# Score masks before the last two multiplications of a group, and GpSimd's two scalings of a unit's q before two different steps

## The chip, the cores and the metric

The kernel runs on one core of a Trainium2 chip. The metric is device time in microseconds. One core has TensorE (matrix multiplications, called PE in the profile), VectorE (DVE), ScalarE (ACT), GpSimd (POOL) and the queue of SyncE (SP), which here only issues DMAs. Each engine works through its own instructions in the order in which the program lists them, and waits for other engines where the program says so.

## The reference

Everything is float32 at the end; the weights come in as float64.

```python
def _attn_ref(q, k, v):                      # (8, 8, 576, 64)
    B, H, S, D_ = q.shape
    scores = np.matmul(q, k.transpose(0, 1, 3, 2)) / np.sqrt(D_)
    gamma = 1.0 - 2.0 ** (-5.0 - np.arange(H, dtype=np.float32))
    rel = np.arange(S)[:, None] - np.arange(S)[None, :]
    Dmat = np.where(rel >= 0, gamma[:, None, None] ** rel[None], 0.0)
    return np.matmul(scores * Dmat[None], v)

def _moe_ref(x, w1, w2, w3, w_out):          # x: (4608, 512)
    h = (x @ w1) * (x @ w2) @ w3             # 512 -> 1024 -> 1024
    return h @ w_out                         # 1024 -> 512
```

The attention is causal with a decay by head and no softmax. Its output, heads side by side, is the x of the second block.

## The kernel before

**Attention.** The work is cut into 20 units: four pairs of batches (`NB2`) by five chunks of the sequence (`NC`; the first has 64 rows, the others 128). The decay is split into a factor on q and a factor on v, so a unit needs a scaled q and a scaled v. For a unit, `score` (L224) multiplies q and k on TensorE into four PSUM tiles `sc`, and VectorE multiplies each by the causal mask into `pm` (L236). `state` (L240) adds k^T v to a running state, and `pv` (L278) multiplies the state and the masked scores into the attention's output, which ScalarE copies out to `xT`. Units 5 to 9 and 12 to 19 bring q in as 32 x 32 blocks: `load_blocks` (L160) issues 16 small DMAs on SP, `scale_blocks` (L175) scales the tile `bl_q` on GpSimd, one instruction (L181) for each of the pair's two batches, and `front_blocks` (L185) transposes it on VectorE (L190).

**Feed-forward.** The tokens of two batches make three tiles of 384. The two first products are made with Strassen's scheme, for the later half of the tokens twice nested: `up2` (L1037) is one of 14 steps (2 halves of the width by 7 outer products) for a pair of token tiles. A step issues eight matmul groups into three PSUM tiles (`up` twice, `seed` once); ScalarE copies and VectorE adds (L1072, L1070) take them out into `cc`, and GpSimd adds parts of `cc` to others (L1065). `next_forms` (L957) issues the DMA of a later step's weights, `ra<-kept` (L961), on GpSimd's queue, into a ring of three slots. The end of a step, its last matmul group, is held in `behind` and put into the next step by `finish`. When both factors of a part are ready, `multiply` (L1024) multiplies them on VectorE into `ab` (L1032), so many as its argument allows; `results` keeps what is left. `down` (L632) takes `ab` and makes the last product, Strassen's seven products of 128 tokens by 256 columns (`po`, L651, w3 and w_out having been multiplied together before), with sums on VectorE (L614 to L620, L655, L699, L701).

**Order.** The order is written by hand; `nc`'s instructions stand on each engine as the Python emits them. The last loop runs over g from 10 to 19. In each round `work(n)` takes n entries of `todo`: 14 `up2` and then three `down` for each pair of token tiles. `dealt = [3, 4, 4, 3, 3, 7, 7, 3, 7, 7]` says how many in each round, so groups 13, 16 and 19 end with the last `up2` of a pair and groups 14 and 17 consist of the three `down`. `aside`, `beside` and `loads` are lists from which steps take one entry each: transposes, v's scalings on ScalarE, k's loads. A round ends with `pv(g)`, at groups 13, 16 and 19 (`ready`) with `finish()` and `multiply()`, then the load of v and `state(g + 1)`, `score(g + 1)`; at the ready groups `token_forms` then prepares the next pair's sums.

**PSUM.** In this part `acc` has five tiles for `up`, `sc`, `xps` and `po`, and `seed` has two. A tile is taken again once its last reader is done: the second product of the `down` that follows a score takes the tile of the first `sc`, and so waits for the first mask.

Of the kernel before, what the change touches and what calls it, by code (L numbers as in the profile page):

```python
# [19 lines left out]
def kernel(  # L20
# [66 lines left out]
    def load(g, names, engine=nc.sync):  # L87
        i, c = divmod(g, NC)
        sz = sizes[c]
        src = {"k": k, "q": q, "v": v}  # L90
        for nm in names:
            t = pools["ld"].tile([P, 2 * H, D], F32, tag="ld_" + nm, name="ld_" + nm)
            engine.dma_start(
                t[:sz], src[nm][2 * i:2 * i + 2, :, starts[c]:starts[c] + sz, :].rearrange("b h p d -> p (b h) d"))
            live[nm, g] = t
# [27 lines left out]
    for c in (0, slice(1, NC)):  # L123
        n = short if c == 0 else P
# [35 lines left out]
    def load_blocks(g, nm):  # L160

        i, c = divmod(g, NC)
        n = sizes[c] // BL
        t = pools["ld"].tile([P, 2 * NP, P // BL, BL], F32, tag="ld_q", name="bl_" + nm)
        src = {"k": k, "q": q}[nm][2 * i:2 * i + 2].rearrange("b (p a) s d -> a (b p) s d", a=2)
        for a in range(2):
            for f in range(D // BL):
                part = (a * (D // BL) + f) * BL
                for m in range(n):
                    s0 = starts[c] + m * BL  # L170
                    nc.sync.dma_start(t[part:part + BL, :, m, :],  # L171
                                      src[a, :, s0:s0 + BL, f * BL:(f + 1) * BL].rearrange("m r x -> r m x"))
        live["bl_" + nm, g] = t

    def scale_blocks(g):  # L175
        c = g % NC
        n, n0 = sizes[c] // BL, starts[c] // BL
        t = live["bl_q", g]
        for b in range(2):
            part = t[:, b * NP:(b + 1) * NP, :n, :]  # L180
            nc.gpsimd.tensor_tensor(  # L181
                out=part, in0=part, in1=gqs[:, :, n0:n0 + n].unsqueeze(3).to_broadcast([P, NP, n, BL]),
                op=ALU.mult)

    def front_blocks(g, names="kq"):  # L185
        c = g % NC
        n = sizes[c] // BL
        for nm in names:
            dst = pools["fr"].tile([P, 2, NP, P], F32, tag=nm + "T", name=nm + "T", bufs=1 if nm == "k" else 2)
            nc.vector.transpose(  # L190
                dst[:, :, :, :sizes[c]].rearrange("p b m (n x) -> p (b m) n x", x=BL),
                live["bl_" + nm, g][:, :, :n, :])
            live[nm + "T", g] = dst

    def scale(g, nm, scalar=False, engine=nc.gpsimd):
        c = g % NC
        sz = sizes[c]
        t, gam = live[nm, g], {"q": gq, "v": gk}[nm]
        t = t[:sz].rearrange("p (b h) d -> p b h d", b=2)
        if scalar:  # L200
            for h in range(H) if scalar is True else scalar:
                nc.scalar.mul(t[:, :, h, :], t[:, :, h, :], gam[:sz, c, h:h + 1])
            return
        engine.tensor_tensor(
            out=t, in0=t, in1=gam[:sz, c].unsqueeze(1).unsqueeze(3).to_broadcast([sz, 2, H, D]), op=ALU.mult)

    def front(g, names="kq"):
        c = g % NC
        sz = sizes[c]
        for nm in names:  # L210
            src = live[nm, g]
            dst = pools["fr"].tile([P, 2, NP, P], F32, tag=nm + "T", name=nm + "T",
                                   bufs=1 if nm == "k" and g >= NC else 2)
            for b in range(2):
                tp = acc.tile([P, NP, P], F32, tag="acc", name="tp")
                for p in range(NP):
                    h = b * H + 2 * p
                    nc.tensor.transpose(tp[:, p, :sz],  # L218
                                        src[:sz, h:h + 2, :].rearrange("p a d -> p (a d)"),
                                        ident[:sz, :sz])  # L220
                nc.scalar.copy(dst[:, b, :, :sz], tp[:, :, :sz])
            live[nm + "T", g] = dst
# [350 lines left out]
    g = 0  # L573
# [53 lines left out]
    def ahead(x, y, n=3):  # L627
        todo_sums = pair_of(x, y)[2]
        for _ in range(min(n, len(todo_sums))):
            aside.append(todo_sums.pop(0))  # L630
# [389 lines left out]
    def finish():  # L1020
        while behind:
            behind.pop(0)()

    def multiply(most=2 * len(order)):  # L1024
        while results and most:
            gr, h, f, b, z, s = results.pop(0)
            m = groups[gr][s]
            if ("ab", *every[m]) not in live:
                live["ab", *every[m]] = ffn.tile([P, 2 * KF, TB], F32, tag="ab", name="ab")
            ab = live["ab", *every[m]].rearrange("p (q i) t -> p q i t", i=4)[:, 2 * h:2 * h + 2, 2 * f + b, :]  # L1030
            v = z.rearrange("p (m s) w t -> p m s w t", s=2)[:, :, s]
            nc.vector.tensor_mul(ab, v[:, :, 0, :], v[:, :, 1, :])  # L1032
            if s == 0:
                free.append(z)
            most -= 1
# [94 lines left out]
    def add_group(gr):  # L1130
        X, Y = groups[gr]
        todo.extend((up2, gr, n) for n in range(14))
        todo.extend([(down, (X, 0), (X, 1)), (down, (X, 2), (Y, 2)), (down, (Y, 0), (Y, 1))])

    def work(n):
        while n > 0 and todo:
            fn, *args = todo.pop(0)

            nxt = next((x for x in todo if x[0] in real), None)
            if nxt and nxt[0] is down:  # L1140
                if fn is down:
                    args.append(nxt[1:])
                else:
                    ahead(*nxt[1:], 1 if fn is up2 else 3)
            if g == G and not todo:
                fn(*args, last=True)
            else:
                fn(*args)
            n -= 1
            while todo and todo[0][0] not in real:  # L1150
                todo.pop(0)[0]()

    g = NC
    scale_blocks(NC)
    scale(NC, "v")
    front(NC, "k")
    front_blocks(NC, "q")
    state(NC)
    score(NC)
    scale_blocks(NC + 1)  # L1160
    in_blocks = [u >= 2 * NC - 3 for u in range(G)] + [False] * 2
    first_pair = range(NC, 2 * NC - 1)
    for g in first_pair:
        n = (1, 1, 2, 2)[g - NC]
# [43 lines left out]
    g = 2 * NC - 1  # L1208
# [9 lines left out]
    g = 2 * NC  # L1218
# [15 lines left out]
    for g in range(2 * NC, G):  # L1234
        n = dealt[g - 2 * NC]
        if g + 1 < G:
            q_blocks = g > 2 * NC
            if not q_blocks:
                beside.extend(lambda j=j: scale(g + 1, "q", range(j, j + H // 2)) for j in (0, H // 2))
            tail = {3: 0, 4: 1, 7: 3}[n]  # L1240
            work(n - 2 - tail)
            beside.extend(lambda j=j: scale(g + 1, "v", range(j, j + H // 2)) for j in (0, H // 2))
            if q_blocks:
                scale_blocks(g + 1)
            for nm in "qk":
                blocks_in = q_blocks if nm == "q" else g + 1 not in whole
                if blocks_in:
                    aside.append(lambda nm=nm: front_blocks(g + 1, nm))
                work(1)
                while aside:  # L1250
                    aside.pop(0)()
                if not blocks_in and nm == "k":
                    while loads:
                        loads.pop(0)()
                    front(g + 1, "k" if q_blocks else "kq")
                if g + 2 < G and not (nm == "k" and g + 2 in whole):
                    load_blocks(g + 2, nm)
            work(tail)
            for left in (loads, beside):
                while left:  # L1260
                    left.pop(0)()
        else:
            work(n)
        pv(g)()
        if g in ready:
            finish()
            multiply()
        if g + 2 < G:
            load(g + 2, "v", nc.gpsimd)
            if (g + 2) % NC != NC - 1:  # L1270
                loads.append(lambda g=g: load(g + 2, "k", nc.gpsimd))
        if g + 1 < G:
            state(g + 1)
            score(g + 1)
        if g in ready:
            add_group(ready[g])
            token_forms(ready[g])
    g = G
# [44 lines left out]
```

## Time and profile before

| | |
|---|---|
| median of three runs | 831.94 us (831.66 to 832.31) |
| the profiled execution | 832.77 us |
| its span, first to last instruction | 831.0 us |
| instructions | 15815 |
| granted TensorE clock | 0.999 |
| VectorE, ScalarE, GpSimd busy | 547.6, 291.8, 222.3 us |
| L1032, multiplications on VectorE in the last loop | 64, median 0.55 us |
| L236, masks of 128x512 there | 32, mean 0.68 us |
| L181, scalings of q on GpSimd there | 16, mean 1.03 us |
| L1065, additions on GpSimd there | 108, mean 1.00 us |
| L961, `ra` issued on GpSimd there | 51, mean 0.57 us |

The rows from L1032 on are from the groups of the stretch from 380 to 800 us, which holds groups 11 to 19; group 10 begins at about 366 us. A row of the profile names line, engine and operation, then the tiles written and read; "idle before" is the time that the engine stood still ahead of the instruction, with who ended it. GpSimd's DMA issues take GpSimd's time[...]; SP's issues, about 0.45 us each, take only SP's.

### The profile page before, as it was taken

The page shows a single profiled execution, that of the slowest core. Times are in us where ns is not written, and L with a number is a line of the kernel's source. Part 1 is how long each engine was busy: PE and PEld are TensorE (multiplying, and loading weights), DVE is VectorE, ACT ScalarE, POOL GpSimd, SP SyncE. Part 2 cuts the span into 40 slices and gives each one's busy share as a digit, 9 for nine tenths or more (in the row PEclk, how much of TensorE's full clock was granted, in tenths as well). Part 3 has the DMA queues.
Part 4 walks back from the last instruction along what each step waited for, and adds up shares of the span by engine and source line. Part 5 has one row for each costly group of instructions (what it writes and reads, how often), then busy time and mean ns, then how long its engine had stood idle before and what let it go on. Part 6 is the DMA issues. An engine that isn't in the chain of part 4 may idle for free.

```text
span 831.0 us, 15815 instructions
## 1 busy us (share of the span) xinstructions
PE 817.5 (98%) x6117; PEld 737.0 (89%) x6117; DVE 547.6 (66%) x962; ACT 291.8 (35%) x609; POOL 222.3 (27%) x258
## 2 busy tenths in 40 slices
PE   8999999999999999999999999999999999999998
PEld 8889999744888998889999889998889998899987
DVE  4899999993544568754657755677745667646653
ACT  4787556572021111255443024341034331033300
POOL 1000000001303332125547015565006460045600
PEclk9999999999999999999999999999999999999999
DMA  9995454446237665988786347978245453146401
GB/s 191 226 224 137 79 131 134 117 126 104 99 66 195 113 151 186 266 264 206 200 228 184 92 88 209 240 224 217 56 92 180 163 191 114 36 149 214 141 26 51
DMA packets 196812, 126.96 MB, mean 153 GB/s; under 512 B 157848, under 2 KB 178456, under 8 KB 196736
## 3 DMA queue, kind: packets, MB, share of 16 engines
q1 hardware_dynamic: 168560, 50.40, 29.6%
q0 software_dynamic: 12480, 65.67, 24.3%
q10 hardware_dynamic: 15696, 9.87, 4.5%
q8 instruction: 48, 0.79, 0.4%
q14 instruction: 28, 0.23, 0.1%
HBM read 103.62 MB, written 22.28 MB: 152 GB/s over the span
## 4 chain that ended last, share of the span: by engine, by line
PE 89%; DVE 6%; DMA 2%; issue 1%; SPq 1%; ACT 1%; ACTq 0%; POOL 0%; DVEq 0%; POOLq 0%
PE po L651 24%; PE up L1060 17%; PE up L528 14%; PE seed L1060 13%; PE ps L477 7%; PE xps L299 3%; PE sc L233 3%; PE xps L274 2%; PE tp L218 2%; PE st L255 1%; SPq L171 1%; DVE pm L236 1%; DVE ab L1032 1%; PE idle L131 1%; DMA ld_v<-in_v_dram 1%
## 5 line engine op out<-in xcount | busy, mean ns | idle before, releaser
L651 PE MATMUL po<-w3o,ab 128*128 128x256 f32 x552 | 125.0, 381 | 2.3 <-DVE ot L655 1.0
L651 PEld LDWEIGHTS po<-w3o,ab 128*128 128x128 f32 x552 | 103.7, 190 | 18.9 <-DVE ot L655 2.5
L1065 POOL TENSOR_TENSOR cc<-cc 128x384 f32<-128x384 f32 x112 | 109.3, 1002 | 3.8 <-ACT cc L1083 2.4
L1072 DVE TENSOR_TENSOR cc<-seed,cc 128x384 f32<-128x384 f32 x88 | 48.7, 553 | 69.0 <-PE seed L1060 59.3
L181 POOL TENSOR_TENSOR bl_q<-bl_q,gqs 128x512 f32<-128x512 f32 (+1 forms) x26 | 26.0, 1020 | 185.8 <-DMA bl_q<-in_q_dram 182.3
L1060 PE MATMUL up<-xT,ra 128*128 128x192 f32 x384 | 73.7, 328 | 0.1
L528 PE MATMUL up<-xT,wA 128*128 128x192 f32 x384 | 70.7, 328 | 1.0 <-DVE xT L496 1.0
L236 DVE TENSOR_TENSOR pm<-sc,mask 128x512 f32<-128x512 f32 (+1 forms) x80 | 45.4, 627 | 35.1 <-PE sc L233 35.1
L1072 DVE TENSOR_TENSOR cc<-up,cc 128x384 f32<-128x384 f32 x88 | 48.5, 551 | 30.2 <-PE up L1060 21.8
L533 DVE TENSOR_TENSOR c<-up,c 128x384 f32<-128x384 f32 x80 | 44.1, 552 | 36.7 <-PE up L528 35.7
L651 PE MATMUL po<-wB,forms 128*128 128x256 f32 x288 | 65.4, 379 | 0.7 <-DVE pm L236 0.7
L528 PEld LDWEIGHTS up<-xT,wA 128*128 128x128 f32 x384 | 63.3, 190 | 2.4 <-PE up L528 1.2
L1060 PEld LDWEIGHTS up<-xT,ra 128*128 128x128 f32 x384 | 63.7, 190 | 1.4 <-DMA ra<-kept 0.4
L961 POOL DMA_DIRECT2D ra<-kept x54 | 30.5, 565 | 118.7 <-PE seed L1060 93.8
L651 PEld LDWEIGHTS po<-wB,forms 128*128 128x128 f32 x288 | 54.6, 190 | 8.4 <-DVE pm L236 1.1
L1079 ACT COPY seed<-up 128x384 f32<-128x384 f32 x56 | 25.9, 463 | 100.2 <-PE up L1060 56.6
L477 PE MATMUL ps<-wo,w3T 128*128 128x512 f32 x128 | 55.1, 592 | 0.0
L1060 PE MATMUL up<-ra 128*128 128x192 f32 x288 | 54.7, 326 | 0.0
L477 PEld LDWEIGHTS ps<-wo,w3T 128*128 128x128 f32 x128 | 24.3, 190 | 30.1 <-issue 29.7
L1060 PE MATMUL seed<-e,ra 128*128 128x192 f32 x256 | 50.9, 329 | 0.0
L1060 PEld LDWEIGHTS up<-ra 128*128 128x128 f32 x288 | 48.1, 190 | 0.1
L528 PE MATMUL up<-T,wS 128*128 128x192 f32 x256 | 46.7, 326 | 1.4 <-DVE wS L149 1.4
(134 smaller groups left out, 1479.1 us busy)
## 6 DMA issues: line engine op xcount, KB each, us to landing
ra<-kept POOLq DMA_DIRECT2D x54, 896.0 KB, 4.9
raw<-in_moe_w_dram SPq DMA_DIRECT2D x72, 128.0 KB, 3.0
bl_q<-in_q_dram SPq DMA_DIRECT2D x192, 32.0 KB, 3.3
out_dram<-ot ACTq DMA_DIRECT2D x41, 128.0 KB, 2.3
bl_k<-in_k_dram SPq DMA_DIRECT2D x136, 32.0 KB, 3.5
raw<-in_moe_w_dram SPq DMA_DIRECT2D x16, 256.0 KB, 5.4
ld_k<-in_k_dram SPq DMA_DIRECT2D x8, 512.0 KB, 6.1
raw<-in_moe_w_out_dram SPq DMA_DIRECT2D x32, 128.0 KB, 2.8
```

Of the source, the lines that this page charges most:

```text
L181: nc.gpsimd.tensor_tensor(out=part, in0=part, in1=gqs[:, :, n0:n0 + n].unsqueeze(3).to_broadcast([P, NP, n, BL]), op=ALU.mult)
L233: nc.tensor.matmul(sc[j][:sz, p, :sz], kT[hs, b, p, :sz], qT[hs, b, p, :sz], start=True, stop=True)
L236: nc.vector.tensor_mul(pm[:sz, b, j, :, :sz], sc[j][:sz, :, :sz], mask[:sz, :sz].unsqueeze(1).to_broadcast([sz, NP, sz]))
L477: nc.tensor.matmul(ps, live["w3T", ft][:, g, :], live["wo"][:, g, :], start=(g == 0), stop=(g == KF - 1))
L528: nc.tensor.matmul(ps[:, w, :], a[:, w, r, :], b[:, r, :], start=(new and w == r == 0), stop=(w == r == 1), skip_group_check=True)
L533: nc.vector.tensor_add(c[:, to], ps, c[:, sb])
L651: nc.tensor.matmul(ps[nm], a[A][:, f, :], live["W"][B][:, f, :], start=(f == 0 and not on), stop=(f == NP - 1), skip_group_check=True)
L961: engine.dma_start(ring[n % 3], kept[n % 14 // 7][nm])
L1060: nc.tensor.matmul(ps[:, w, :], weight_of(slot, a, w), B[b], start=(new and w == 0), stop=True, skip_group_check=True)
L1065: nc.gpsimd.tensor_tensor(out=o, in0=o, in1=i, op=ALU.add)
L1072: nc.vector.tensor_add(c[:, j], ps, with_add[:, j])
L1079: nc.scalar.copy(p6, p1)
```

## The change

There are two edits, both in the last loop. In the first, `scale_blocks` gets the argument `batches`, and the loop calls it twice: the scaling of the first batch's half of the next unit's q is issued one step ahead of where both stood, and the second stays. For groups of three and four steps the first one now stands ahead of all steps of the group, for groups of seven behind the first. In the second, at the ready groups, only two of the multiplications left (there are four) are issued ahead of v's load, `state` and `score`; the other two come after the four masks.

```diff
-    def scale_blocks(g):
+    def scale_blocks(g, batches=range(2)):
...
-        for b in range(2):
+        for b in batches:
             part = t[:, b * NP:(b + 1) * NP, :n, :]
...
             tail = {3: 0, 4: 1, 7: 3}[n]
-            work(n - 2 - tail)
+            work(n - 3 - tail)
+            if q_blocks:
+                scale_blocks(g + 1, (0,))
+            work(1)
             beside.extend(lambda j=j: scale(g + 1, "v", range(j, j + H // 2)) for j in (0, H // 2))
             if q_blocks:
-                scale_blocks(g + 1)
+                scale_blocks(g + 1, (1,))
             for nm in "qk":
...
         pv(g)()
         if g in ready:
             finish()
-            multiply()
+            multiply(2)
         if g + 2 < G:
             load(g + 2, "v", nc.gpsimd)
...
             state(g + 1)
             score(g + 1)
         if g in ready:
+
+            multiply()
             add_group(ready[g])
             token_forms(ready[g])
```

In the order of instructions nothing is added or removed on any engine. On GpSimd eight scalings move ahead, each past one `ra` issue, in six of the eight groups past one to three others (additions or k's load) as well. On VectorE, at the ends of groups 13 and 16, two multiplications move behind four masks.

## The prediction

> **What bounds the kernel now.** I read the page's first part and its chain, then who waits for whom on TensorE, then the timelines of TensorE, VectorE and GpSimd around the two late waits that this list names.
>
> ```profile
> PE 817.5 (98%) x6117; PEld 737.0 (89%) x6117; DVE 547.6 (66%) x962; ACT 291.8 (35%) x609; POOL 222.3 (27%) x258
> PE 89%; DVE 6%; DMA 2%; issue 1%; SPq 1%; ACT 1%; ACTq 0%; POOL 0%; DVEq 0%; POOLq 0%
> ```
> ```profile
> PE po L651 <- DVE pm L236: 1.5, 2, 0.8
> ...
> PE seed L1060 <- DVE cc L1072: 0.4, 1, 0.4
> ```
>
> TensorE is busy for 817.5 of 831.0 us and carries 89% of the chain. A change that adds no matrix work and takes none away can win only what is left in TensorE's gaps. The second fence is from the list of TensorE's waits (total, times, longest). The wait for masks (L236) has two cases, but one, 0.65 us at 327.37, lies before the edited loop starts at about 366 us. The other is the row at 576.14 below.
>
> ```profile
> 573.30 1.99 PE L651 MATMUL po<-w3o,ab 128*128 128x256 f32 x8
> 576.14 3.72 PE L651 MATMUL po<-w3o,ab 128*128 128x256 f32 x16 [0.85 <-DVE pm L236]
> ...
> 570.82 4.67 DVE L1032 TENSOR_TENSOR ab<-cc 128x384 f32<-128x384 f32 x4
> 575.41 2.47 DVE L236 TENSOR_TENSOR pm<-sc,mask 128x512 f32<-128x512 f32 x4
> 577.81 0.67 DVE L618 TENSOR_TENSOR forms<-ab 128x512 f32<-128x512 f32 x1
> ...
> 571.49 0.55 POOL L961 DMA_DIRECT2D ra<-kept  x1
> 572.06 2.07 POOL L181 TENSOR_TENSOR bl_q<-bl_q,gqs 128x512 f32<-128x512 f32 x2
> 574.07 1.23 POOL L93 DMA_DIRECT2D ld_k<-in_k_dram  x1
> ```
>
> These are the timelines (start, length, engine, line) where group 16 ends. Group g is the loop's g; its end is `pv`, `state`, `score`. The scores are ready at about 573.4, the first mask starts at 575.41, and the second product of `down` (8 matmuls a product) waits for the PSUM tile that this mask frees. Ahead of the masks stand four multiplications L1032 that take 4.67 us where four of the median 0.55 take about 2.
>
> ```profile
> 542.67 2.05 POOL L181 TENSOR_TENSOR bl_q<-bl_q,gqs 128x512 f32<-128x512 f32 x2
> 544.74 0.57 POOL L961 DMA_DIRECT2D ra<-kept  x1
> 545.34 1.96 POOL L1065 TENSOR_TENSOR cc<-cc 128x384 f32<-128x384 f32 x2
> ...
> 543.57 4.16 DVE L1032 TENSOR_TENSOR ab<-cc 128x384 f32<-128x384 f32 x2
> 547.65 0.54 DVE L1072 TENSOR_TENSOR cc<-seed,cc 128x384 f32<-128x384 f32 x1
> ...
> 547.16 0.92 PE L1060 MATMUL up<-xT,ra 128*128 128x192 f32 x4
> 547.91 0.81 PE L1060 MATMUL up<-e,ra 128*128 128x192 f32 x4
> 549.17 0.92 PE L1060 MATMUL seed<-u,ra 128*128 128x192 f32 x4 [0.45 <-DVE cc L1072]
> ```
>
> This is the other wait, inside group 16. Two multiplications take 4.16 us instead of 1.0 while GpSimd goes from the scalings over a DMA issue into the next additions. The additions L1072 that empty the `seed` tile come late, and TensorE waits.
>
> ```profile
> L1032 DVE TENSOR_TENSOR ab<-cc x64: 536/550/3271, 379.9 to 794.8; 128x384 f32<-128x384 f32 x64
> ```
>
> The query by line gives minimum, median and maximum of L1032: 550 ns against 3271 at worst.
>
> **What the Trainium skill says.** "SBUF — State Buffer", section "Who interferes with whom": VectorE and GpSimd share a pair of SBUF ports, a VectorE instruction with two SBUF inputs contends with a GpSimd instruction that reads SBUF, and the later one is blocked fully; with at most one SBUF input it isn't. The trace agrees: L1032 reads two SBUF operands and grew to 3.27 us beside L181, whereas L1072, with one operand from PSUM, kept 0.56 us at 391.46 beside the same scalings. It shows more than one instruction's length, since both scalings and the additions behind them went first. "GPSIMD Engine Reference", in its table, says the same of the shared interface. So where a scaling stands matters, though GpSimd is only 27% busy.
>
> **Part 1: masks ahead of the last multiplications (ends of groups 13 and 16; at 19 no score follows, so nothing moves).** Nothing is added or removed. VectorE's order becomes 2 multiplications, 4 masks, 2 multiplications, then the sum S2 (L618) as before. The program's order shows no wait lost, no instruction changed; the third product of `down` waits for ScalarE's copy alone, the fourth for S2.
> Group 16's end: in the worst case the second multiplication is held as before until GpSimd's chain frees it. Scalings and DMA keep their sum (ld_v to 571.49, then scaling 1.0, issue 0.57, scaling 1.0), so it ends at about 574.5, and the first mask at 574.5 + 0.65 = 575.15, in place of 576.1. Product 2's own time is 573.30 + 8 x 0.216 + 0.1 = 575.13. (0.216 is the spacing of starts at 455.40 to 460.82: 24 matmuls, 5.42 us with two such 0.1 us starts.) TensorE's three products took 579.70 - 573.30 = 6.40 us here and 460.82 - 455.40 = 5.42 at group 13's end without the wait: 0.98 us to win, less up to 0.1 for the 575.15 mask: 0.9 to 1.0.
> What is late next: the two multiplications left, 577.0 to 578.0, then S2 to 578.7. The fourth product, moved up by 0.95, wants S2 at 579.70 - 0.95 = 578.75. It just fits. If the hold at 571.28 is shorter, there is more room.
> Group 13's end: no gap now; the masks may move up by 1.0 us and win nothing. The two late multiplications end at about 458.6, S2 at 459.3, wanted at 460.82: nothing lost.
>
> **Part 2: the first scaling one step earlier (eight units, groups 11 to 18).** One of two L181 (1.05 us each; 0.6 to 0.9 for the short unit) goes ahead of the step's DMA issue `ra` (L961), the step's additions L1065, and in some groups ld_k (L93).
> Does it wait for its data? q's block DMAs are issued on SP well before: for group 11 by 373.95, with the longest landing of any, 7.8 us, by 381.8, and the scaling's new place is 383.1, behind ld_v. At groups 12, 13, 15, 16, 17, 18 the last issue plus 7.8 is also earlier than the new place (the tightest: 561.0 + 7.8 = 568.8 against 571.5). Only in group 14 is it not: the issues run to 453.6 and the scaling starts at 455.38 now. There `ra`, the other scaling, ld_k stand behind a wait of some 1.5 us; but that `ra` feeds the first steps after three `down`s, at about 497 or later, and lands in 5 to 9 us. Hidden, with some 35 us to spare.
> Elsewhere GpSimd idles where the scaling goes: 4.6 us before `ra` at 387.75, 3.8 at 412.99, 3.9 at 438.11, 4.6 at 503.82, 2.8 at 540.19, 7.4 at 624.32. VectorE does masks or nothing with two SBUF inputs there. Cost 0; without that cover 1.05 us a unit on `ra`.
> Gain in group 16: only one scaling remains at 542.67 to 543.7; then GpSimd is idle until `ra` at 544.74 (its rhythm of 4.55 us a step, 540.19 to 544.74, doesn't change). The two multiplications fit into 543.7 to 544.7. The step from `ra` at 544.74 to `ra` at 550.39 is 5.65 us, 1.10 over the rhythm. Of this, the late landing of `ra` keeps its part: after 546.23 come four matmuls of 0.1625 (0.65), so 546.88 was due and 547.16 came, 0.28, and 0.10 more in the restart (four matmuls from 547.16 take 0.75). The rest, 1.10 - 0.38 = 0.72, goes. Bounds: 0.72 at most, 0 if the multiplications are held through the next additions all the same. I take 0.7.
>
> **The sum.** 0.95 + 0.7 = 1.65 us. The profiled execution, 832.77 us (span 831.0 and 1.8 around it), becomes about 831.1, its span 829.4. The median of the three runs, 831.94, lies 0.83 below the profiled one, so I carry over the difference: 830.3 us.
>
> **Rivals.**
> A (0.55): both waits go: 830.3. For it: both slow groups of L1032 lie against scalings. It spreads over 829.8 to 830.8 with the sizes above and the runs' own spread of 0.3.
> B (0.18): only the masks' wait goes, the multiplications are still held by the chain: 831.94 - 0.95 = 831.0. For it: at 571.28 a multiplication was held though the scaling began at 572.06 only.
> C (0.12): only the step's wait goes, since S2 or the first multiplications become the wait in the mask's place: 831.2. For it: S2 fits by less than 0.1 us.
> D (0.15), slower: the multiplications that stay ahead of the masks are the ones that GpSimd's chain holds. Scaling, `ra`, scaling, ld_k now run on behind ld_v with nothing between. If they hold VectorE through ld_k's issue, group 16's first mask ends at 575.3 + 0.45 + 0.65 = 576.4, 0.3 later than now; at group 13's end the chain ends at about 458.0, the mask at 459.1, and product 2 wants it at 457.2: 1.9 lost where nothing is lost now. If both early multiplications are held one after another, 0.5 more each. With the step's 0.7 won: 831.94 + 0.3 + 1.9 + 1.0 - 0.7 = 834.4. It decides once the hold at group 13 lasts past 456.1. Against it: there the multiplications start at 454.22, before the data of the scaling are in.
>
> **How the numbers follow.** 0.2%, about what can be told from no change here, is 1.66 us, or 830.28: the forecast lies on that line. Half of A is beyond it, and so is a further share if the late `ra` at 547.16 also goes (0.38 more). Faster: 0.46 (most of A). Same: 0.40 (rest of A, B, C). Slower: 0.14 (D). The range from 829.7 to 832.0 holds A, B and C, with a margin above for the runs' spread, and leaves D out; A alone is 829.8 to 830.8.
>
> **What would show it.** Right: no TensorE gap behind masks after 366 us, L1032's maximum down from 3271 to about 1000 in group 16's middle (the one at its end may stay), a step rhythm of 4.55 to 4.95 us at 544.74, S2 before the fourth product. Wrong: a gap of the fourth product behind L618, the 4.16 us pair still there, a new wait behind L236 at 457, or `ra` landing late because its issue came after the scaling.

## The result, and the profile after

The change made the kernel faster by about two microseconds, as forecast: median 830.14 us (828.74 to 832.3, 22 runs) against 832.09 us for the kernel before (831.04 to 834.55, 22 runs), ratio 0.9977 with a 95% interval of 0.9971 to 0.9983. A second measurement beside later experiments gave 0.9973 (0.9962 to 0.9983). The forecast was 830.3 us, 1.65 us less than its median of before; 1.95 us came.

The page of after, busy time and chain of waits by engine:

```profile
PE 817.5 (98%) x6117; PEld 737.2 (89%) x6117; DVE 543.2 (65%) x962; ACT 291.8 (35%) x609; POOL 223.0 (27%) x258
PE 86%; DVE 5%; DMA 4%; issue 2%; SPq 2%; ACT 1%; POOL 0%; ACTq 0%; DVEq 0%; POOLq 0%
```

TensorE's work is the same 817.5 us, as it must be. VectorE has exactly the same 962 instructions and is busy 4.4 us less (547.6 before). This is mostly time in which multiplications were held and counted as busy: the 64 of L1032 add up to 41.8 us before and to 37.0 after.

TensorE's waits of over 0.15 us in the last loop (from 385 us), after (total, times, longest):

```profile
PE up L1060 <- DMA ra<-kept: 0.7, 2, 0.5
PE po L651 <- DVE ot L655: 0.6, 1, 0.6
PE po L651 <- DVE ab L614: 0.5, 1, 0.5
```

The two waits on which the prediction rested, for the mask L236 and for the sum L1072, are not in this list. Instead the late landing of `ra` grew, from one gap of 0.12 us to two that make 0.7. This profiled execution is one of the longer ones of its kernel (832.11 us, its span 830.4), so the gain is not to be read from its span.

At the end of group 16, the timelines of after (start, length, engine, line, tiles, count), TensorE first:

```profile
573.21 5.45 PE L651 MATMUL po<-w3o,ab 128*128 128x256 f32 x24
578.49 2.75 PE L651 MATMUL po<-wB,forms 128*128 128x256 f32 x12
```
```profile
570.73 2.87 DVE L1032 TENSOR_TENSOR ab<-cc 128x384 f32<-128x384 f32 x2
573.52 2.47 DVE L236 TENSOR_TENSOR pm<-sc,mask 128x512 f32<-128x512 f32 x4
575.91 1.01 DVE L1032 TENSOR_TENSOR ab<-cc 128x384 f32<-128x384 f32 x2
576.96 0.69 DVE L618 TENSOR_TENSOR forms<-ab 128x512 f32<-128x512 f32 x1
```
```profile
571.42 1.07 POOL L181 TENSOR_TENSOR bl_q<-bl_q,gqs 128x512 f32<-128x512 f32 x1
572.42 0.59 POOL L961 DMA_DIRECT2D ra<-kept  x1
573.03 1.47 POOL L181 TENSOR_TENSOR bl_q<-bl_q,gqs 128x512 f32<-128x512 f32 x1
```

The three products take 578.49 - 573.21 = 5.28 us without a gap; before they took 6.40. That is 1.12 us less: the mask's wait and, 0.1 of it, the restart after it. VectorE still has a held multiplication (2.87 us for two), but the masks start at 573.52 instead of 575.41, and S2 (L618) ends at 577.65, 0.84 us before the fourth product wants it.

Inside group 16, the same three engines:

```profile
546.52 0.81 PE L1060 MATMUL seed<-ra 128*128 128x192 f32 x4
547.78 0.92 PE L1060 MATMUL up<-xT,ra 128*128 128x192 f32 x4 [0.45 <-DMA ra<-kept]
548.54 0.81 PE L1060 MATMUL up<-e,ra 128*128 128x192 f32 x4
549.19 0.81 PE L1060 MATMUL seed<-u,ra 128*128 128x192 f32 x4
```
```profile
543.85 1.10 DVE L1032 TENSOR_TENSOR ab<-cc 128x384 f32<-128x384 f32 x2
544.87 0.54 DVE L1072 TENSOR_TENSOR cc<-seed,cc 128x384 f32<-128x384 f32 x1
```
```profile
543.00 1.05 POOL L181 TENSOR_TENSOR bl_q<-bl_q,gqs 128x512 f32<-128x512 f32 x1
545.03 0.59 POOL L961 DMA_DIRECT2D ra<-kept  x1 [0.98 <-PE seed L1060]
...
550.30 0.57 POOL L961 DMA_DIRECT2D ra<-kept  x1 [2.70 <-PE seed L1060]
```

One scaling in place of two, and GpSimd then idles 0.98 us: the pair of multiplications takes 1.10 us instead of 4.16, and `seed` at 549.19 follows its predecessor without a gap.

One of the named signs did not come. The step from one `ra` to the next takes 550.30 - 545.03 = 5.27 us, and 4.55 to 4.95 was named. The 0.72 over the rhythm of 4.55 is the late `ra`: four matmuls of 0.1625 from 546.52 end at 547.17, the next started at 547.78, 0.61 later, and its restart takes 0.1. The moved scaling doesn't make this `ra` late. It was issued 540.48 - 535.93 = 4.55 us after the one before it, as it was before the change (540.19 - 535.64).

### The profile page after: what moved, and what is told of

The parts are those of the page before. It is cut to its first block, busy times and chain, and to the rows that moved or that the text cites. A ratio compares the mean times of both kernels' runs of the same rounds, so it can differ in the third digit from the quotient of the medians.

```text
span 830.4 us, 15815 instructions
## 1 busy us (share of the span) xinstructions
PE 817.5 (98%) x6117; PEld 737.2 (89%) x6117; DVE 543.2 (65%) x962; ACT 291.8 (35%) x609; POOL 223.0 (27%) x258
## 4 chain that ended last, share of the span: by engine, by line
PE 86%; DVE 5%; DMA 4%; issue 2%; SPq 2%; ACT 1%; POOL 0%; ACTq 0%; DVEq 0%; POOLq 0%
PE po L651 24%; PE up L1060 16%; PE up L528 15%; PE seed L1060 12%; PE ps L477 7%; PE xps L299 3%; PE sc L233 3%; DMA ra<-kept 2%; DMA bl_k<-in_k_dram 2%; PE xps L274 2%; SPq L171 2%; PE tp L218 2%; PE st L255 1%; DVE pm L236 1%; PE idle L131 1%
## 5 line engine op out<-in xcount | busy, mean ns | idle before, releaser
L1072 DVE TENSOR_TENSOR cc<-seed,cc 128x384 f32<-128x384 f32 x88 | 48.7, 553 | 70.4 <-PE seed L1060 61.7
L1072 DVE TENSOR_TENSOR cc<-up,cc 128x384 f32<-128x384 f32 x88 | 48.5, 551 | 31.4 <-PE up L1060 23.0
L236 DVE TENSOR_TENSOR pm<-sc,mask 128x512 f32<-128x512 f32 (+1 forms) x80 | 45.4, 627 | 34.6 <-PE sc L233 34.5
```

The source lines that it names most:

```text
L236: nc.vector.tensor_mul(pm[:sz, b, j, :, :sz], sc[j][:sz, :, :sz], mask[:sz, :sz].unsqueeze(1).to_broadcast([sz, NP, sz]))
L1072: nc.vector.tensor_add(c[:, j], ps, with_add[:, j])
```

## The experiments

All ratios are to the kernel before, run beside it on the same chip. The rows x_, y_ and z_ come from three chips, so compare their ratios rather than their medians. Since the time at which the last loop is reached turned out to vary between executions, I also give the loop's length in the profiled execution of each: from the row of unit 11's score (L233, the end of group 10; 383.24 us before) to the end of the last matmul (826.04 + 1.89 = 827.93 us before). Before, it is 444.69 us. This length varies too: by 0.55 us between the two profiles of the change itself.

| kernel | median, us | ratio (95%) | loop, us |
|---|---|---|---|
| the change | 830.14 | 0.9977 (0.9971 to 0.9983) | 443.92 |
| the change again (z_after) | 829.76 | 0.9973 (0.9962 to 0.9983) | 443.37 |
| x_masks: second edit alone | 830.40 | 0.9983 (0.9971 to 0.9994) | 443.64 |
| x_scal: first edit alone | 831.68 | 0.9996 (0.9984 to 1.0008) | 444.92 |
| x_one: second edit, one scaling moved | 829.57 | 0.9975 (0.9964 to 0.9985) | 442.91 |
| y_scal14: first edit without group 14 | 831.20 | 0.9988 (0.9979 to 0.9997) | 443.59 |
| y_noscale: before, four scalings left out | 829.67 | 0.9974 (0.9966 to 0.9982) | 443.13 |
| x_ldk: the change, k's loads on SP | 853.26 | 1.0262 (1.0247 to 1.0277) | - |
| y_ldk16: the change, one of k's loads on SP | 830.37 | 0.9985 (0.9977 to 0.9994) | 442.74 |
| y_best | 829.08 | 0.9971 (0.9963 to 0.9978) | 441.26 |
| z_kt | 828.34 | 0.9965 (0.9952 to 0.9978) | 441.48 |
| z_mul0 | 828.72 | 0.9964 (0.9951 to 0.9978) | 441.53 |

My theory: two gaps on TensorE, one for each edit, both made by GpSimd's scalings holding VectorE. The rivals: only one of the edits counts (B and C of the prediction), or many of the moves count a little.

**The second edit alone.**

```diff
         if g in ready:
             finish()
-            multiply()
+            multiply(2)
...
+        if g in ready:
+            multiply()
             add_group(ready[g])
```

> The kernel before with the second edit alone: two of the four multiplications behind the masks, both scalings where they were. Theory (two separate waits, one for each edit): the wait for the mask at the end of group 16 goes (about 1.0 us), the one on the seed tile in group 16 stays with its pair of multiplications at about 4 us: 1.0 us faster than before, ratio 0.9988. Rival (the scalings' place is all that counts, the masks' wait is only its consequence): no faster than 0.3 us.

TensorE's waits in the loop, second edit alone:

```profile
PE seed L1060 <- DVE cc L1072: 0.8, 1, 0.8
...
```

No wait for a mask is in the list, the one on `seed` is there, and the loop is 1.05 us shorter, as expected. The time, 0.9983, lies 0.4 us lower than expected, inside the interval. The rival falls.

By the time alone this kernel and the whole change can't be told apart (0.9983 and 0.9977, with overlapping intervals). That the first edit adds something is shown by the traces. The step in group 16 from one `ra` to the next takes 5.65 us before and here. In the ten other profiles with a loop length above it takes 4.55 to 5.27 us, depending on when `ra` lands.

**The first edit alone.** The diff is the change without its last two parts.

> The kernel before with the first edit alone: the first scaling a step earlier, all multiplications ahead of the masks. Theory: the wait on the seed tile in group 16 goes (0.7 us); at the end of group 16 the two scalings now have a DMA issue between them, so the held multiplication comes free after the first one, and the mask's wait of 0.85 us shrinks to about 0.5: in all 1.0 to 1.2 us faster than before, ratio 0.9986. Rival (only the masks' order counts): within 0.3 us of before, the 4 us pair still there. Rival (splitting the scalings cures both waits, the masks' order adds nothing): as fast as the whole change, 1.9 us.

This was not what came: 0.9996, no difference that can be told, with the expected 0.9986 at the edge of the interval. The wait on `seed` is gone, but the list has two waits for masks, 1.4 us together. One is new, at the end of group 13. TensorE, VectorE and GpSimd there, first edit alone (about 1.9 us later on its clock than before):

```profile
457.31 1.99 PE L651 MATMUL po<-w3o,ab 128*128 128x256 f32 x8
459.90 3.72 PE L651 MATMUL po<-w3o,ab 128*128 128x256 f32 x16 [0.60 <-DVE pm L236]
463.46 2.75 PE L651 MATMUL po<-wB,forms 128*128 128x256 f32 x12
```
```profile
456.14 3.11 DVE L1032 TENSOR_TENSOR ab<-cc 128x384 f32<-128x384 f32 x4
459.17 2.47 DVE L236 TENSOR_TENSOR pm<-sc,mask 128x512 f32<-128x512 f32 x4
```
```profile
456.92 0.71 POOL L181 TENSOR_TENSOR bl_q<-bl_q,gqs 128x256 f32<-128x256 f32 x1 [1.20 <-DMA bl_k<-in_k_dram]
457.58 0.59 POOL L961 DMA_DIRECT2D ra<-kept  x1
458.19 0.64 POOL L181 TENSOR_TENSOR bl_q<-bl_q,gqs 128x256 f32<-128x256 f32 x1
```

The same place before:

```profile
455.40 5.58 PE L651 MATMUL po<-w3o,ab 128*128 128x256 f32 x24
460.82 3.62 PE L651 MATMUL po<-wB,forms 128*128 128x256 f32 x16
```
```profile
454.22 2.38 DVE L1032 TENSOR_TENSOR ab<-cc 128x384 f32<-128x384 f32 x4
```
```profile
455.38 1.71 POOL L181 TENSOR_TENSOR bl_q<-bl_q,gqs 128x256 f32<-128x256 f32 x2 [1.03 <-DVE ab L1032]
```

The four multiplications took 2.38 us before and take 3.11 now. The two scalings, pulled apart by the DMA issue, meet two different multiplications, and each holds one (0.97 and 1.28 us). Before, one multiplication was held (0.98 us), and then the second scaling waited (0.93 us). The three products take 463.46 - 457.31 = 6.15 us now and took 460.82 - 455.40 = 5.42 before, so 0.73 us is lost in this profile. With the second edit they take 5.28 here, so that 5.42 held a small wait already.

The other mask's wait, at the end of group 16, didn't shrink either (0.84 us): the second scaling held a later multiplication for 1.4 us. In the whole change the masks stand ahead of the multiplications that are held so, and neither loss comes to bear. That the two parts add up was my mistake; the second covers a loss that the first leaves.

A test of this one move:

```diff
-            if q_blocks:
+            if q_blocks and g != 14:
                 scale_blocks(g + 1, (0,))
...
-                scale_blocks(g + 1, (1,))
+                scale_blocks(g + 1, (1,) if g != 14 else range(2))
```

> The first edit alone, but unit 15's two scalings (group 14) stay together where they were. The first edit alone won the seed tile's wait (0.7 us) and paid a new wait of 0.73 us for the first mask at the end of group 13, where the short unit's scalings now run among the four multiplications. Theory (that one move makes the wait): the mask's wait at 457 is gone, the one at the end of group 16 stays at 0.85, and it is 0.7 us faster than before, ratio 0.9991. Rival (the wait at 457 comes from the run's DMA times, not from the move): it is there again.

The new wait is gone (one wait for masks is left, 0.8 us), and the step in group 16 takes 4.55 us, 1.10 less than before: 0.72 for the `seed` wait and 0.38 for a late `ra` that wasn't late in this execution. The ratio, 0.9988, agrees, but its interval overlaps that of the first edit. Nor does the profile refute the rival, that the wait comes from the run's DMA times. In the profiles in which all four multiplications stand ahead of the masks (y_noscale is described below), group 13's end looks like this:

| profile | unit 15's scalings | first one starts, from the first product's start | three products, us |
|---|---|---|---|
| y_scal14 | together | +0.49 | 5.28 |
| before | together | -0.02 | 5.42 |
| y_noscale | together | -0.33 | 5.84 |
| first edit alone | apart | -0.39 | 6.15 |

The first scaling starts about 0.25 us after the last landing of q's blocks, in each of the four, so the move doesn't shift it. The earlier it fell among the multiplications, the more was lost, and 0.56 us was lost in y_noscale with the scalings together. The last two rows, where the landing is nearly the same, leave 0.31 us for the move, from one profile each. How much of the first edit's missing gain is due to the move and how much to the landing stays open.

**One moved scaling is enough.**

```diff
+            if q_blocks and g == 16:
                 scale_blocks(g + 1, (0,))
...
+                scale_blocks(g + 1, (1,) if g == 16 else range(2))
```

> The whole change, but of the eight moved scalings only the one in group 16 moves; in the other groups both stay together. Theory (seven of the eight moves are hidden): the seed tile's wait and the mask's wait both gone, as fast as the whole change within 0.3 us, ratio to before 0.9978; at the end of group 16 one multiplication is held for about 3 us by both scalings and the first mask still comes in time. Rival (all eight moves count, by holding VectorE less): 0.5 us or more slower than the whole change.

0.9975 against 0.9977: the other seven moves bring nothing that the time shows. Of TensorE's waits in the loop only the last two of the list of after are left. One of the seven does shorten a gap too small for that list: at the end of group 16, where unit 18's scalings are now together again and hold one multiplication for 3.27 us, the three products take 5.46 us, against 5.28 in the whole change.

**What the scalings cost.** The kernel before with the calls for units 17 and 18 left out, two scalings each:

```diff
-            if q_blocks:
+            if q_blocks and g not in (16, 17):
                 scale_blocks(g + 1)
```

> The kernel before with the scalings of units 17 and 18 left out (so part of q's scaling is left out; the transposes follow as before). It asks what the scalings at these two places cost. Theory (VectorE is held by the scalings and by what runs behind them without a gap): no multiplication of the loop above 1.0 us, both waits gone, 1.7 us faster than before, ratio 0.9979. Rival (GpSimd's DMA issues hold VectorE by themselves): the multiplication at about 571 stays held for over 1 us beside v's load, ra and k's load.

VectorE and GpSimd at the end of group 16 without the scalings:

```profile
569.73 1.96 DVE L1032 TENSOR_TENSOR ab<-cc 128x384 f32<-128x384 f32 x4
571.60 2.48 DVE L236 TENSOR_TENSOR pm<-sc,mask 128x512 f32<-128x512 f32 x4
```
```profile
569.21 1.20 POOL L93 DMA_DIRECT2D ld_v<-in_v_dram  x1 [3.51 <-PE xps L299]
570.41 0.55 POOL L961 DMA_DIRECT2D ra<-kept  x1
570.94 1.17 POOL L93 DMA_DIRECT2D ld_k<-in_k_dram  x1
```

Four multiplications in 1.96 us, right beside three DMA issues: the issues by themselves hold nothing, and the rival falls. Both waits of before are gone. The longest L1032 of the loop is 0.97 us here, at the end of group 13, where unit 15's scalings remained; there this execution had a mask's wait of 0.3 us too, against the expectation. So the kernel before stands on an edge at that place, and the second edit removes this as well. It fits with x_masks and the whole change having won a little more than the gaps of one profile, though three profiles don't tell how often it occurs.

One thing stays open. The multiplication that is held before begins at 571.28, and its usual 0.55 us would end at 571.83, ahead of the scaling's start at 572.06. In after, the one at 570.73 would end at 571.28, ahead of 571.42. Without the scalings none is held there, so they are the cause, but the traces don't show why the hold begins before them.

**The late `ra`.**

```diff
-                loads.append(lambda g=g: load(g + 2, "k", nc.gpsimd))
+                loads.append(lambda g=g: load(g + 2, "k", nc.sync))
```

> The whole change, and k's loads of the last loop issued on SP's queue instead of GpSimd's. It asks why the ring's DMA (ra) lands late in group 16 (6.9 us before, 7.3 us after, where 4.9 is usual) and stops TensorE there at 547. Theory: it stands behind k's 512 KB in the same queue; on another queue ra lands within 6 us and the TensorE gap behind DMA at 547 goes: 0.4 to 0.7 us faster than the whole change. Rival (all 16 DMA engines are full there, from whatever queue): ra as late as before, no gain, or a loss where k's load now meets the blocks of q and k on SP.

Much slower, and for a reason that only the rival's last clause touches. TensorE's waits in its loop:

```profile
PE st L255 <- DMA ld_k<-in_k_dram: 19.6, 2, 9.9
```

At the three `down` of groups 14 and 17, SP's queue stands at blocks of k that wait for a transpose; k's load behind them is issued at 497.57, needed at about 495, and lands in 6.9 to 8.2 us. Moved for group 16 alone:

```diff
-                loads.append(lambda g=g: load(g + 2, "k", nc.gpsimd))
+                loads.append(lambda g=g: load(g + 2, "k", nc.sync if g == 15 else nc.gpsimd))
```

> The whole change, and only unit 17's k, loaded in group 16, on SP's queue. Moving all of k's loads there lost 10 us twice, where SP's queue stood behind blocks that waited for a transpose; in group 16 it doesn't. Theory (ra is late there as it stands behind k's 512 KB in GpSimd's queue): ra issued at about 540 lands within 6 us and TensorE's gap behind DMA at 547 goes, 0.4 to 0.7 us faster than the whole change, ratio to before 0.9970. Rival: as late as before, 0.9977.

The gap behind `ra` is gone in this profile, as it is in those of x_ldk and y_best, which move this load too. But it is also absent in x_masks, y_scal14, y_noscale and z_kt, which leave the load where it was. The time, 0.9985, is no better than that of the change, and the forecast of 0.9970 lies outside its interval. Whether k's load makes `ra` late is not settled by this.

**A version beyond both.** One more gap in the list of after stands behind VectorE's sum L655 at the third `down`, where k's transpose (1.24 us) is queued ahead of it.

```diff
+                late = nm == "k" and g in (14, 17)
-                if blocks_in:
+                if blocks_in and not late:
                     aside.append(lambda nm=nm: front_blocks(g + 1, nm))
                 work(1)
+                if late:
+                    front_blocks(g + 1, nm)
```

> The change with one moved scaling alone (unit 17), unit 17's k on SP's queue, and in groups 14 and 17 the transpose of k at the end of the third down instead of within it. The last product's wait for the sum L655 at 610 (0.57 us) and 490 stands behind that transpose of 1.24 us. Theory (these are three separate gaps on TensorE): another 0.6 to 0.8 us for the transposes and 0.4 for k's load, 829.57 to about 828.5, ratio to before 0.9960. Rival (the score after it waits for the later transpose instead): no gain over the whole change.

> The second edit, unit 17's moved scaling alone, and k's transposes of groups 14 and 17 at the end of the third down; k's loads all on GpSimd's queue. Theory (the sum L655 at 490 and 610 stood behind the transpose): both TensorE gaps gone, 0.3 and 0.8 us, so 1.0 us faster than the whole change; the gap behind the late ra at 547 may stay, up to 0.4 us. Ratio to before 0.9967.

TensorE at that place in z_kt:

```profile
603.26 1.89 PE L651 MATMUL po<-wB,ab 128*128 128x256 f32 x8
604.99 1.89 PE L651 MATMUL po<-w3o,ab 128*128 128x256 f32 x8
```

No gap is left. The same place before:

```profile
609.97 1.99 PE L651 MATMUL po<-w3o,ab 128*128 128x256 f32 x8 [0.57 <-DVE ot L655]
```

The loops of y_best and z_kt are over 3.2 us shorter than that of before. z_kt came as forecast (0.9965 for 0.9967), while y_best gained less: its forecast of 0.9960 lies outside its interval. z_kt has a median of 828.34 us where the change, measured beside it, has 829.76, but the intervals of the ratios overlap. The nearest to a proof by time is y_best against y_ldk16, measured beside it: 829.08 against 830.37 us, with intervals that barely touch. y_ldk16 has k's load on SP too, but neither the later transposes nor the seven scalings back in their places. So the step beyond the change is shown by the gaps, and the time only supports it.

```diff
         if g in ready:
             finish()
-            multiply(2)
+            multiply(0)
```

> The kernel above with all four multiplications behind the masks instead of two. Theory (two of them are enough for the mask to come in time, and the fourth product waits for S2 behind all four in any order): no difference within 0.3 us; S2 ends as late as with two. Rival (the held multiplication ahead of the masks still costs): the second product starts up to 0.1 us earlier, or the held multiplication now delays S2 and the fourth product waits for it.

Multiplications by line in z_mul0 (minimum, median, maximum in ns):

```profile
L1032 DVE TENSOR_TENSOR ab<-cc x64: 539/552/889, 378.2 to 790.0; 128x384 f32<-128x384 f32 x64
```

With all four behind the masks the longest takes 889 ns (z_kt has 3269), and the time is the same, 0.9964 and 0.9965. The traces show a small difference, though. S2 ends 4.29 us after the first product's start and not as late as in z_kt (5.30), and the three products take 5.28 us in place of 5.46. So the multiplication held ahead of the masks still cost 0.18 us, as the rival had it, too little for the medians.

## Why the prediction was right, and where not

The mechanism and the main case A held. Point by point:

- *The bound.* TensorE's work stayed 817.5 us; the gain came from its gaps alone.
- *Part 1.* Priced at 0.9 to 1.0 for the end of group 16. With the second edit alone the three products there take 5.47 us in place of 6.40, so 0.93. That is my worst case: the first mask is ready 1.86 us after the first product's start, and 1.85 was computed. In the whole change the DMA issue now between the scalings lets the held multiplication go after the first one, and 1.12 is won. S2, which I had fitting by under 0.1 us, has 0.84 to spare there. "Group 13's end: no gap now" was not quite right: I took the 5.42 us there as the time without a wait, and it is 5.28.
- *Part 2, gain.* 0.72 at most predicted. The `seed` row follows at once in every kernel with unit 17's scaling moved, but the step shrank by 5.65 - 5.27 = 0.38 us in the profile of after, and by 1.10 in y_scal14. The late `ra`, which the sum kept at its size of before, decides which. Group 14's scaling waits for its data (1.37 us idle before it after) and `ra` behind it comes at 456.14 with no one waiting, as said.
- *Part 2, cost.* Put at 0, and in the whole change no loss is seen. But for group 14 the working looked only at the `ra` behind the scaling, and not at VectorE's queue beside it. The scalings there start when q's blocks have landed, among the multiplications at the end of group 13. In the first edit alone TensorE then lost 0.73 us more than in the profile of before, and only the other edit hides this. It is D's mechanism (a multiplication ahead of the masks held at group 13's end), with 0.73 instead of 1.9 us, and most of it may be due to when the blocks landed. In the whole change D didn't come.
- *The late `ra`.* Left as it was in the sum. At 547 it was a gap of 0.12 us before, 0.45 in the profile of after, 0.26 in that of z_after, 0.13 in x_one, none in x_masks. It varies between executions, and no run ties it to the change.
- *Size.* 1.65 forecast, 1.95 measured, with an interval of about 1.4 to 2.4. That the two lie so close is in part luck. The loop is shorter by only 0.77 and 1.32 us in the change's two profiles, as `ra` landed later there than the sum had it, while group 13's end, which the sum left out, lost 0.14 us in the profile of before and 0.56 in y_noscale, which is the kernel before at that place. How these two average over the runs is not known.

## What to carry to other kernels

Where one engine is busy 98% of the time, look for its few gaps, and then at what stands ahead of the awaited instruction in the other engine's queue: putting the awaited one first is safer than making the work ahead of it shorter. When an operation of GpSimd is moved, lay it beside VectorE's timeline too, not only into a hole of its own queue. And test the parts of a change alone, since one part can pay for a gap that another part hides.

## What the runs showed that I had not expected

- At the end of group 16, two scalings issued with nothing between them held one multiplication through both (3.27 us); inside group 16, two additions did the same (2.66 us). With a DMA issue between the scalings the multiplication was let go after the first (2.40 us), and without the second edit the second scaling then held a later one (1.40 us). But it is no rule: at the end of group 13 before, two shorter scalings with nothing between them let the multiplication go after the first (0.98 us), and the second scaling took 0.93 us, where it takes about 0.61 alone.
- The later scaling itself took 1.47 us instead of 1.05 in that contest.
- The stretch up to unit 11's score, whose code no kernel here changes, ended anywhere from 381.37 to 385.18 us in the profiles behind the table. This is more than the whole gain, so single executions of such kernels say little about it, and the gaps in the loop say more.
